# Gated FFT / GEGLU training step: twelve row tiles transposed by DMA, dO scaled on VectorE, the first FFT pieces and sorts spread out

## The chip, the cores and the metric

The kernel runs on 1 core of one Trainium2 chip. The metric is device time in microseconds (us) of one execution, as the median of several runs. The core has TensorE (PE in the profile, its weight loads PEld), VectorE (DVE), ScalarE (ACT), GpSimd (POOL) and SyncE (SP). SP, ACT and POOL can issue DMAs; 16 DMA engines move the data.

## The reference, cut to what matters

Forward and backward of a mix of two branches on one sequence of S = 2048 rows, D = 576 columns, F = 4608:

```python
g = sigmoid((x * gate_w).sum(-1, keepdims=True))
a = irfft2(rfft2(x) * (w_r + 1j*w_i), s=(S, D))            # branch A
b = (gelu(x @ w_gate) * (x @ w_up)) @ w_down               # branch B
out = g * a + (1 - g) * b
# outputs: out and the gradients of x, w_r, w_i, w_gate, w_up, w_down, gate_w for grad_out (dO)
```

Both branches start from `x`, so the gradient of `x` is a sum of both and of the gate's. Everything is bf16 at the borders.

## The kernel before, in words

**Tiles.** The 2048 rows are 16 row tiles of 128 rows; tile t holds rows 16p + t, p being the partition. `xn` and `dB` hold x and dO as loaded (rows on partitions); `xT` and `dOT` hold them transposed (columns on partitions) in five column chunks: chunks 0 to 3 are columns 0 to 511, chunk 4 holds the last 64 columns of two neighbouring tiles, one in each half of the partitions.

**Phase 1** (to about 890 us) is a loop over 18 groups g of 256 columns of F, each in 4 steps m of four row tiles. I count the steps through, step n = 4g + m (`pr` in the code). A step does:

- on PE, `z = dO w_down^T` (L449, L454), then `xy = x [w_gate, w_up]` in two halves (L458, L465);
- on ACT, `da = (1-g) z` (L477), the evacuations of xy (L484 to L487) and the sigmoids of the GELU (L512, or L515 and L516);
- on DVE, the product chain: `H_ew1` (L492 to L496, called as soon as xy is evacuated) and `H_ew2` (L507 to L540: L523 to L533), which waits for the sigmoid. They make `A` and `dH`, which SP stores to DRAM (L537) for phase 2;
- on PE, the weight gradient matmuls of the *group before* (`W_units`, L556 to L619): L577 multiplies `A` with `dB`, L595 and L609 multiply `xn` with `dH`. Their results are evacuated by ACT or DVE (L546) and stored by POOL.

**Way in.** In group 0 the transposes of x and dO are still to be done. `titems` (L396 to L413) gives three items for four row tiles: item 0 transposes column chunks 0 and 1 on PE against an identity (L404, 8 matmuls into PSUM) and copies them to `xT` or `dOT` (L411); item 1 does the same for chunks 2 and 3; item 2 does chunk 4 (L410, 4 matmuls). Step 0 does tiles 0 to 7, step 1 prepares x tiles 8 to 11 (`x1`) and, at its end, dO tiles 12 to 15 (`do2[0]`; the rest of `do2` is done inside the z of the next step, L994 and L1033), step 2 prepares x tiles 12 to 15. `gate(k)` (L423) computes g for four tiles from `xT`; `da` of the same tiles needs it.

**L577 needs dO scaled.** Before the first L577, `dB` is multiplied by 1-g in place, tile by tile (`scale_dB`, L961 to L966). Four tiles are one call: tiles 0 to 3 and 8 to 11 on ACT in step 4 (L1046, L1058), 4 to 7 on DVE in step 4 (L1063), 12 to 15 on ACT in step 5 (L1043). The first L577 come in step 5: two units over tiles 0 to 7 and then the same two over tiles 8 to 15.

**FFT of branch A.** The FFT pieces are spread over the steps: 64 forward pieces for x and dO, `u1` (L639, evacuated by ACT at L642) and `u2` (L653, evacuated by ACT at L659, followed by 17 small DVE operations and a store), then the middle pieces (L758, L836). All of them use the one PSUM tile `pz`, which z uses too. How many have run by the end of a step is set by `want` (L933): for steps 0 to 8 by the table `FIRST` (L930), here 3 by the end of step 7 and 7 by the end of step 8; after that evenly up to step 65. A piece u1 needs its row of x sorted by residue classes (`sort`, L703, one ACT copy of 128x576). The first three sorts are on ACT in step 4 (L1064), the others follow each second piece (L901). The sine tables of the FFT are made by `run_late` in step 6 (L1083): two ACT table loads and seven sines in one row on ACT.

**Queues.** Each engine runs its instructions in the order of the program. SP's DMAs share eight semaphores in rotation with ACT's: the issue of one waits until the DMA eight places before it has landed. At the start SP issues `wdn`, dO tiles 0 to 3, x 0 to 3, the group's two weight blocks, then dO and x alternately, four tiles each; then two small DMAs for a table (L110, L111; the second reads what the first wrote), then the weights of group 1 (`load_w(1, ...)`, L343 to L350, with two DMA transposes of `B_w_down`), then the stores of step 0. The four 64-column tails of group 0's weights are issued from ACT's queue (L345 with `tails`).

**Phase 2** reloads `A` and `dH` by DMA transposes (L1124) and computes b, the gradient of x and the inverse FFT. The change does not touch it.

Of the kernel before, what the change touches and what calls it, by code (L numbers as in the profile page):

```python
# [19 lines left out]
S, D, DF = 2048, 576, 289  # L20
P, T = 128, 16
# [7 lines left out]
FG = 256  # L29
# [8 lines left out]
LO, HI = slice(0, 64), slice(64, 128)  # L38
# [23 lines left out]
def iotas(nc, res, unit):  # L62
    tb = Tables()
    G, V = nc.gpsimd, nc.vector
    kw = dict(allow_small_or_imprecise_dtypes=True)
    tb.halfpi = res.tile([P, 1], F32, name="halfpi")
    V.memset(tb.halfpi[:], math.pi / 2)
    tb.pi = res.tile([P, 1], F32, name="pi")
    V.memset(tb.pi[:], math.pi * EPS_SCALE)
    tb.warm = res.tile([P, 1], F32, name="warm")  # L70
    nc.scalar.activation(tb.warm[:], tb.halfpi[:], ACT.Sigmoid)
    tb.lrow = unit([LQ], F32, name="lrow")
    G.iota(tb.lrow[:], pattern=[[1, LQ]], base=0, channel_multiplier=0, **kw)
    tb.dcol = res.tile([P, 6], F32, name="dcol")
    for k, (r, step, n) in enumerate(((1, 1, 2), (0, 0, 1), (5, -1, 3))):
        k0 = (0, 2, 3)[k]
        G.iota(tb.dcol[:, k0:k0 + n], pattern=[[step, n]], base=r, channel_multiplier=6, **kw)
    tb.late = []
    tb.Rt = []
    return tb  # L80
# [211 lines left out]
def kernel(  # L292
# [4 lines left out]
    nc = tc.nc  # L297
    LD = nc.sync
    ST = nc.gpsimd
# [27 lines left out]
    xT = hres.tile([P, 5, T, P], BF16, name="xT")  # L327
    dOT = hres.tile([P, 5, T, P], BF16, name="dOT")
    xn = wstack.enter_context(tc.tile_pool(name="pxn", bufs=1)).tile([P, T, D], BF16, name="xn")
    dB = wstack.enter_context(tc.tile_pool(name="pdB", bufs=1)).tile([P, T, D], BF16, name="dB")  # L330

    wts = {}

    def load_w(g, part, tails=LD):

        fsl = slice(g * FG, (g + 1) * FG)
        if g not in wts:
            wts[g] = (wpool.tile([P, 5, 2 * FG], BF16, tag="wgu", name="wgu"), wpool.tile([P, 5, FG], BF16, tag="wdT", name="wdT"))
        if part == 0:
            wgu = wts[g][0]  # L340
            for w, c0 in ((B_w_gate, 0), (B_w_up, FG)):
                cols = slice(c0, c0 + FG)
                LD.dma_start(wgu[:, 0:4, cols], w[0:512, fsl].rearrange("(r p) f -> p r f", p=P))  # L343
                for r in (LO, HI):
                    tails.dma_start(wgu[r, 4, cols], w[512:D, fsl])  # L345
        elif part == 1:
            LD.dma_start_transpose(wts[g][1][:, 4:5, :], B_w_down[fsl, DCH[4][0]:D])
            LD.dma_start_transpose(wts[g][1][:, 0:4, :], B_w_down[fsl, 0:512])
        else:
            LD.dma_start(wts[g][1][LO, 4, :], wts[g][1][HI, 4, :])  # L350

    def load_x(t0):
        LD.dma_start(xn[:, t0:t0 + 4, :], x_v[:, t0:t0 + 4, :])
# [10 lines left out]
    load_do(0, 2)  # L364
    load_do(2, 2)
    load_x(0)
    load_w(0, 0, nc.scalar)
    for k in range(1, 4):
        load_do(4 * k)
        load_x(4 * k)  # L370
    tb = iotas(nc, res, unit)

    ew = wstack.enter_context(tc.tile_pool(name="ew", bufs=2))
    keepA = wstack.enter_context(tc.tile_pool(name="keepA", bufs=6))
# [21 lines left out]
    def titems(src, dst, t0, ps, copies, n=4):  # L396

        def item(k, cs):
            def f():
                tp_ = ps[k](BF16).rearrange("p (j t m) -> p j t m", j=2, t=4)  # L400
                for j, c in enumerate(cs):
                    for tt in range(n):
                        if c < 4:
                            nc.tensor.transpose(tp_[:, j, tt, :], src[:, t0 + tt, eo(c)], ident[:])  # L404
                        elif n < 4:
                            for r in (LO, HI):
                                nc.tensor.transpose(tp_[r, 0, tt, :], src[:, t0 + tt, 512:D], ident[:])
                        else:
                            c0 = (t0 + tt) * D + (512, D - P)[tt % 2]
                            nc.tensor.transpose(tp_[:, 0, tt, :], src[:].rearrange("p t d -> p (t d)")[:, c0:c0 + P], ident[:])  # L410
                copies[k](dst[:, cs[0]:cs[0] + len(cs), t0:t0 + n, :], tp_[:, 0:len(cs), 0:n, :])  # L411
            return f
        return [item(k, cs) for k, cs in enumerate(((0, 1), (2, 3), (4,)))]  # L413
# [75 lines left out]
    def H_ew1(g, tiles, da):  # L489
        xb, q, hu = tiles  # L490
        s = ewt("s", g)
        V.tensor_scalar(s[:], q[:], A_GELU, 1.0, op0=ALU.mult, op1=ALU.add)  # L492
        V.tensor_tensor(s[:], xb[:], s[:], op=ALU.mult)
        V.tensor_scalar(q[:], q[:], 6.0 * A_GELU * C_GELU, 2.0 * C_GELU, op0=ALU.mult, op1=ALU.add)
        dH = keep.tile([P, 4, 2, FG], BF16, tag="dH", name="dH")
        V.tensor_tensor(dH[:, :, 0, :], da[:], hu[:], op=ALU.mult)  # L496
        return s, dH
# [187 lines left out]
    xq, gq, graw = {}, {}, {}  # L685
# [17 lines left out]
    def sort(dst, t):  # L703
        if t % 2 == 0:
            classes(dst, t // 2)
        if dst is xq:
            nc.scalar.copy(xq[t], xn[:, t, :].rearrange("p (q r) -> p r q", r=6))
        else:
            nc.scalar.activation(gq[t], graw[t // 2][:, t % 2].rearrange("p (q r) -> p r q", r=6), ACT.Copy, scale=g32[:, t:t + 1])
# [150 lines left out]
    VC, AC = V.tensor_copy, nc.scalar.copy  # L860
# [6 lines left out]
    for c in range(6):  # L867
        w = gwr[0:1, eo(c)] if c < 4 else gwr[0:1, 512:D]
# [58 lines left out]
    mid_at = 4 * T + 8  # L927
    NPR = NT // 2
    LASTP = NG * NPR - 7
    FIRST = (0, 0, 0, 0, 0, 0, 0, 3, 7)  # L930
    done = [0]

    def want(pr):  # L933
# [27 lines left out]
    def scale_dB(k, cp):  # L961
        for t in range(4 * k, 4 * k + 4):
            if cp == AC:
                nc.scalar.activation(dB[:, t, :], dB[:, t, :], ACT.Copy, scale=omg32[:, t:t + 1])  # L964
            else:
                V.tensor_scalar(dB[:, t, :], dB[:, t, :], omg32[:, t:t + 1], None, op0=ALU.mult)  # L966

    for g in range(NG):
# [3 lines left out]
        for m in range(NPR):  # L972
# [14 lines left out]
                H_ew2(g, m, tiles, *state)  # L987
            if g == 0:
                def items(src, dst, t, *cp):
                    return titems(src, dst, 4 * t, (pgtile,) * 3, cp) if t < NPR else [None] * 3  # L990
                do1 = items(dB, dOT, 1, VC, VC, VC) if m == 0 else []
                do2 = items(dB, dOT, m + 2, AC, AC, VC)
                x1 = items(xn, xT, m + 1, AC if m else VC, VC, VC)
# [43 lines left out]
            else:  # L1037
                z, xy_full = H_mm(g, m)
                da = H_da(g, m, z)
                for f in inside:  # L1040
                    f()
                if pr == 5:
                    scale_dB(3, AC)  # L1043
                xy = xy_full(0)
                if held:
                    scale_dB(0, AC)  # L1046
                    held.pop()()
                k0 = int(n > 0 and pr > 6 and ready())
                xy0 = xy
# [6 lines left out]
                    H_act(1, xy, tiles, part)  # L1056
                if pr == 4:
                    scale_dB(2, AC)  # L1058
                elif pr == 6:
                    next(makeB)  # L1060
                state += [*H_ew1(g, tiles, da), da]
                if pr == 4:
                    scale_dB(1, VC)  # L1063
                    for t in range(3):  # L1064
                        sort(xq, t)
                elif pr == 5:
                    build_R(nc, tb, unit, 8)
                    build_R(nc, tb, unit, 12)
                side_work(4.4)
# [378 lines left out]
```

## Time and profile before

| what | us |
|---|---|
| median of the 3 runs | 1370.08 |
| lowest, highest of the runs | 1368.88, 1371.35 |
| the profiled execution, its own time | 1368.51 |
| its span (first to last instruction) | 1366.7 |
| PE busy | 1348.3 (99%) |
| DVE busy | 880.7 (64%) |
| ACT busy | 782.4 (57%) |
| DMA transposes issued by SP: the median time on its queue of L347, L348, L1124, L954, L1157 | 1.26, 1.29, 1.41, 1.64, 3.59 |

The profile is of one execution. Busy time is a union of intervals. PE's matmuls are pipelined: a 128x512 matmul is shown with 379 ns, but one starts every 213 ns; so the time that a wait costs PE is read from start to start and is some 0.16 us longer than the idle that is shown. In the timeline a row gives the start in us from the start of the span, the time that it covers, engine, line, operation and count; in brackets stand the idle time before it and who ended it. In a table of stretches each engine's entry is the busy time in that stretch.

### The profile page before, as it was taken

The numbers are of one execution on the slowest core, as the hardware profiler recorded it, in microseconds if no ns is written. First come the engines' busy times: TensorE is split into PE (matmuls) and PEld (weight loads), VectorE is DVE, ScalarE is ACT, GpSimd is POOL, SyncE is SP. The second block draws the span as 40 slices with busy tenths as digits, with TensorE's granted clock in tenths as the row PEclk, the third lists the DMA queues.
The fourth block names the chain that finished last, engine by engine and source line by source line (L and its number), as shares of the span: only waits on it lengthen the run. The fifth ranks groups of instructions, "written<-read, shape, count | busy, mean of one in ns | idle before, by whom it ended". The sixth has DMA issues, their size and how long they took to land.

```text
span 1366.7 us, 27046 instructions
## 1 busy us (share of the span) xinstructions
PE 1348.3 (99%) x10327; PEld 903.6 (66%) x10408; DVE 880.7 (64%) x2348; ACT 782.4 (57%) x1389; POOL 245.8 (18%) x484
## 2 busy tenths in 40 slices
PE   9999999999999999999999999999999999999999
PEld 7556656656656655656655655658888888888887
DVE  7888988988768876786786655525535443545320
ACT  6987888887767777776776666622332322222210
POOL 2001111111314532442441311100000000000000
PEclk9999999999999999999999999999999999999999
DMA  6424444534634644744654648499999778789773
GB/s 221 121 75 124 130 123 125 154 116 118 168 107 114 175 123 110 184 130 111 182 130 128 157 123 173 126 241 219 217 210 198 175 163 163 165 158 175 158 146 74
DMA packets 487128, 205.33 MB, mean 150 GB/s; under 512 B 306803, under 2 KB 479030, under 8 KB 486998
## 3 DMA queue, kind: packets, MB, share of 16 engines
q1 hardware_dynamic: 460660, 168.75, 53.4%
q0 software_dynamic: 14912, 24.24, 6.1%
q10 hardware_dynamic: 11426, 10.61, 3.3%
q8 instruction: 81, 1.33, 0.4%
q14 instruction: 49, 0.40, 0.1%
HBM read 41.04 MB, written 89.11 MB: 95 GB/s over the span
## 4 chain that ended last, share of the span: by engine, by line
PE 94%; ACT 3%; issue 1%; DVE 1%; DMA 0%; SPq 0%; DVEq 0%; ACTq 0%
PE acc L1198 31%; PE wps L595 17%; PE xy L465 17%; PE wps L577 10%; PE z L449 9%; PE wps L609 2%; PE xy L458 2%; PE z L454 2%; PE acc L1251 1%; PE pf L639 1%; PE acc L1261 1%; PE pf L653 1%; ACT dB L964 1%; PE pf L836 1%; PE pf L758 1%
## 5 line engine op out<-in xcount | busy, mean ns | idle before, releaser
L1198 PEld LDWEIGHTS <-pin 128*128 128x128 bf16 x3456 | 334.8, 98 | 83.2 <-issue 1.1
L465 PE MATMUL xy<-wgu,xT 128*128 128x512 bf16 x1081 | 258.0, 379 | 8.5 <-issue 7.1
L595 PE MATMUL wps<-dH,xn 128*128 128x512 bf16 x1142 | 264.4, 379 | 0.5
L595 PEld LDWEIGHTS <-xn 128*128 128x128 bf16 x1152 | 111.1, 98 | 125.0 <-issue 0.6
L465 PEld LDWEIGHTS <-xT 128*128 128x128 bf16 x1152 | 105.8, 98 | 131.9 <-issue 24.8
L602 POOL DMA_DIRECT2D out_dram<-dw x134 | 73.7, 554 | 429.5 <-ACT dw L546 411.9
L577 PE MATMUL wps<-dB,A 128*128 128x288 bf16 x1152 | 149.8, 286 | 0.5 <-ACT dw L546 0.3
L1198 PE MATMUL acc<-wd_all,pin 128*128 128x288 bf16 x1152 | 146.7, 286 | 0.0
L1198 PE MATMUL acc<-wgT,pin 128*128 128x288 bf16 x1152 | 146.6, 286 | 0.0
L1198 PE MATMUL acc<-wuT,pin 128*128 128x288 bf16 x1152 | 146.0, 286 | 0.0
L1263 ACT ACTIVATE yo<-acc 128x288 bf16<-128x288 f32 x64 | 67.4, 1246 | 133.7 <-PE acc L1261 122.3
L449 PE MATMUL z<-wdT,dOT 128*128 128x256 bf16 x1152 | 137.7, 273 | 0.6 <-ACT ve L659 0.6
L577 PEld LDWEIGHTS <-A 128*128 128x128 bf16 x1152 | 112.0, 98 | 34.1 <-issue 0.9
L477 ACT ACTIVATE da<-z,omg 128x256 bf16<-128x256 f32 x288 | 112.1, 472 | 29.6 <-PE z L454 29.5
L449 PEld LDWEIGHTS <-dOT 128*128 128x128 bf16 x1152 | 112.5, 98 | 22.2 <-issue 1.1
L1379 DVE TENSOR_TENSOR b16t<-acc,f32t 128x288 bf16<-128x288 f32 x32 | 14.6, 458 | 171.7 <-PE acc L1198 171.6
L486 ACT CAST xb<-xy 128x512 bf16<-128x512 f32 x144 | 85.1, 591 | 48.6 <-PE xy L465 48.6
L1253 ACT CAST Z<-acc 98x384 bf16<-98x384 f32 x64 | 27.5, 481 | 106.2 <-PE acc L1251 106.2
L487 ACT CAST hu<-xy 128x512 bf16<-128x512 f32 x144 | 87.4, 607 | 0.0
L484 ACT ACTIVATE q<-xy 128x512 bf16<-128x512 f32 x144 | 80.3, 601 | 3.9 <-PE xy L465 3.5
L523 DVE TENSOR_TENSOR xb<-xb,sg 128x1024 bf16<-128x1024 bf16 x48 | 33.1, 690 | 72.5 <-ACT sg L515 72.5
L546 ACT CAST dw<-wps 128x512 bf16<-128x512 f32 x72 | 42.1, 587 | 59.2 <-PE wps L595 58.6
(514 smaller groups left out, 1825.6 us busy)
## 6 DMA issues: line engine op xcount, KB each, us to landing
scr<-dH SPq DMA_DIRECT2D x144, 256.0 KB, 3.4
scr<-A SPq DMA_DIRECT2D x72, 256.0 KB, 2.4
out_dram<-dw POOLq DMA_DIRECT2D x134, 64.0 KB, 1.9
wd_all<-in_B_w_down_dram SPq DMA_DIRECT2D x3, 1728.0 KB, 13.1
out_dram<-dwd POOLq DMA_DIRECT2D x34, 144.0 KB, 3.1
scr_p<-Vt SPq DMA_DIRECT2D x32, 144.5 KB, 2.8
Vp<-scr_p ACTq DMA_DIRECT2D x32, 144.5 KB, 4.3
wgu<-in_B_w_gate_dram SPq DMA_DIRECT2D x18, 256.0 KB, 3.8
```

What stands on the lines that cost most here:

```text
L449: nc.tensor.matmul(zo(t), lhsT=dOT[:, ci, t, :], rhs=wdT[:, ci, :], start=(t % 4 < 2 and ci == 0), stop=False)
L465: nc.tensor.matmul(xy[k][:, t % 2, :], lhsT=xT[:, ci, t, :], rhs=wgu[:, ci, :], start=False, stop=(ci == 3))
L477: nc.scalar.activation(da[:, t, :], z[:, t % 2, t // 2, :], ACT.Copy, scale=omg32[:, 4 * m + t:4 * m + t + 1])
L484: nc.scalar.activation(q[:, h, :], xy[:, :, 0:FG], ACT.Square)
L486: nc.scalar.copy(xb[:, h, :], xy[:, :, 0:FG])
L487: nc.scalar.copy(hu[:, h, :], xy[:, :, FG:2 * FG])
L546: wcopy[0](out, in_)
L577: nc.tensor.matmul(wps[:, :288], lhsT=tl(0, t)[:, fch * P:(fch + 1) * P], rhs=dB[:, t, h * 288:(h + 1) * 288], start=(t == 0), stop=(t == ...
L595: nc.tensor.matmul(wps[:].rearrange("p a b -> p (a b)"), lhsT=xn[:, t, c * P:(c + 1) * P], rhs=kt[t // 4][1][:, t % 4].rearrange("p k f -> ...
L602: wst[0].dma_start(ov[:, c, fsl], dw[:, k, :])
L1198: nc.tensor.matmul(acc[:, :288], lhsT=src[:, r, :], rhs=w_of(r)[:, h * 288:(h + 1) * 288], start=(first and r == 0), stop=(last and r == F ...
L1263: nc.scalar.activation(yv[:, 3 * b:3 * b + 3], ps[:, 0:288].rearrange("p (r q) -> p r q", r=3), ACT.Copy, scale=(SD2, 1.0)[w])
```

## The change

Five things are altered, all of them in the first steps.

1. Chunks 0 to 3 of x tiles 8 to 11, dO tiles 12 to 15 and x tiles 12 to 15 are no longer transposed on PE: twelve DMA transposes of one row tile each (128 rows, 512 columns), issued by SP from DRAM, write `xT` and `dOT`. Four stand behind the load of x tiles 8 to 11, eight behind that of x tiles 12 to 15. Item 2 (chunk 4) of these tiles stays on PE; items 0 and 1 become empty.
2. The tails of group 0's weights go from ACT's queue to POOL's, behind the first iotas.
3. `scale_dB` of tiles 0 to 3 goes from ACT to DVE (step 4, after `H_ew1`, with 4 to 7), that of tiles 12 to 15 from ACT before the xy of step 5 to DVE after the `H_ew1` of step 5. Tiles 8 to 11 stay on ACT.
4. The first three sorts, on ACT in step 4 before, are on ACT in steps 5, 6 and 7, one each, after the evacuations of xy.
5. `FIRST` asks for 1 FFT piece by the end of step 7 and 3 by the end of step 8, in place of 3 and 7. By `want` the new kernel is 3 pieces behind the old one from step 9 to step 30, 1 behind to step 63 and level from step 64.

```diff
-                for r in (LO, HI):
-                    tails.dma_start(wgu[r, 4, cols], w[512:D, fsl])
+                if tails:
+                    for r in (LO, HI):
+                        tails.dma_start(wgu[r, 4, cols], w[512:D, fsl])
...
-    load_w(0, 0, nc.scalar)
+    load_w(0, 0, None)
+    turned_by_dma = {("x", 2), ("do", 3), ("x", 3)}
+
+    def load_turned(v, dst, k):
+        flat = v[0].rearrange("(p t) d -> p (t d)", t=T)
+        for t in range(4 * k, 4 * k + 4):
+            LD.dma_start_transpose(dst[:, 0:4, t, :], flat[:, t * D:t * D + 512])
     for k in range(1, 4):
         load_do(4 * k)
         load_x(4 * k)
+        for n, v, dst in (("do", grad_out, dOT), ("x", A_x, xT)):
+            if (n, k) in turned_by_dma:
+                load_turned(v, dst, k)
     tb = iotas(nc, res, unit)
+    for w, c0 in ((B_w_gate, 0), (B_w_up, FG)):
+        for r in (LO, HI):
+            ST.dma_start(wts[0][0][r, 4, c0:c0 + FG], w[512:D, 0:FG])
...
-    FIRST = (0, 0, 0, 0, 0, 0, 0, 3, 7)
+    FIRST = (0, 0, 0, 0, 0, 0, 0, 1, 3)
...
-                    return titems(src, dst, 4 * t, (pgtile,) * 3, cp) if t < NPR else [None] * 3
+                    if t >= NPR:
+                        return [None] * 3
+                    its = titems(src, dst, 4 * t, (pgtile,) * 3, cp)
+                    return [gap, gap, its[2]] if ("x" if src is xn else "do", t) in turned_by_dma else its
...
-                if pr == 5:
-                    scale_dB(3, AC)
                 xy = xy_full(0)
                 if held:
-                    scale_dB(0, AC)
                     held.pop()()
...
                 if pr == 4:
                     scale_dB(2, AC)
+                elif pr == 5:
+                    sort(xq, 0)
                 elif pr == 6:
                     next(makeB)
+                    sort(xq, 1)
+                elif pr == 7:
+                    sort(xq, 2)
                 state += [*H_ew1(g, tiles, da), da]
                 if pr == 4:
+                    scale_dB(0, VC)
                     scale_dB(1, VC)
-                    for t in range(3):
-                        sort(xq, t)
                 elif pr == 5:
+                    scale_dB(3, VC)
                     build_R(nc, tb, unit, 8)
                     build_R(nc, tb, unit, 12)
```

`gap` is an empty function; `LD` is SP's queue, `ST` POOL's; `VC` and `AC` are the copies of DVE and ACT.

## The prediction

> **What bounds the kernel now.** I read the page first. Its part 1 gives PE's busy time; in part 2 each digit is an engine's busy tenth in one of 40 equal slices; part 4 gives the engines' shares of the chain that ended last.
>
> ```profile
> PE 1348.3 (99%) x10327; PEld 903.6 (66%) x10408; DVE 880.7 (64%) x2348; ACT 782.4 (57%) x1389; POOL 245.8 (18%) x484
> DVE  7888988988768876786786655525535443545320
> ACT  6987888887767777776776666622332322222210
> ...
> PE 94%; ACT 3%; issue 1%; DVE 1%; DMA 0%; SPq 0%; DVEq 0%; ACTq 0%
> ```
>
> PE is busy all the span and carries the chain. So a change pays only where PE loses time, or where it takes work off PE. I looked for these places with PE's rows, start to start: up to step 8 there are waits; from step 9 to the end of phase 1 the same steps return with the same lengths (12.12, 12.42, 12.83, 14.05 us again and again), which only PE's own work explains. So what follows is about the first 106 us. The same engines by stretch, one row a step (steps 2 to 8; after the stretch PE, PEld, DVE, ACT, POOL busy):
>
> ```profile
> 28.60:37.50 8.90, 8.68 (x96) 5.86 (x95) 7.93 (x16) 8.36 (x17) 0.00 (x0) 1.00 0.30 91
> 37.50:43.50 6.00, 5.84 (x44) 3.33 (x42) 5.74 (x11) 4.77 (x14) 0.00 (x0) 1.00 0.42 131
> 43.50:55.00 11.50, 11.41 (x65) 5.81 (x65) 9.92 (x18) 10.63 (x21) 0.00 (x0) 1.00 0.23 70
> 55.00:67.50 12.50, 11.97 (x80) 7.25 (x80) 10.31 (x20) 12.50 (x22) 2.39 (x4) 1.00 0.68 184
> 67.50:81.10 13.60, 13.39 (x113) 8.95 (x113) 12.32 (x29) 11.65 (x24) 1.63 (x3) 1.00 0.38 115
> 81.10:93.10 12.00, 10.86 (x75) 5.89 (x75) 8.22 (x16) 11.97 (x22) 0.88 (x2) 1.00 0.04 14
> 93.10:105.80 12.70, 11.26 (x87) 6.94 (x88) 12.07 (x42) 10.42 (x18) 1.83 (x4) 1.00 0.32 96
> ```
>
> In step 5 ACT is busy all 12.50 us and DVE 10.31; in steps 7 and 8 PE idles 1.14 and 1.44 us. PE's timeline says for whom:
>
> ```profile
> 28.18 0.61 PE L404 MATMUL pf<-ident,dB 128*128 128x128 bf16 x8
> ...
> 66.40 1.26 PE L577 MATMUL wps<-dB,A 128*128 128x288 bf16 x9 [0.17 <-ACT dB L964]
> ...
> 86.91 0.49 PE L639 MATMUL pf<-Rt,xq 128*96 128x128 bf16 x6 [0.46 <-ACT da L477]
> ...
> 93.09 1.91 PE L449 MATMUL z<-wdT,dOT 128*128 128x256 bf16 x16 [0.63 <-ACT ve L659]
> ...
> 103.04 0.49 PE L639 MATMUL pf<-Rt,xq 128*96 128x128 bf16 x6 [1.39 <-ACT ve L659]
> ```
>
> Step 5 waits for the scaled dO (L964). The waits of steps 7 and 8 (0.46, 0.63, 1.39) are for ACT: its sine tables of step 6 (run_late) make it late, and then every FFT piece needs the one `pz` tile emptied. Start to start the last two are worth 0.79 and 1.55 us.
>
> **The change, part by part.** Times are made against the profiled execution, 1368.51 us (span 1366.7 and 1.8 around it); the runs' median is 1.57 above that, so a difference worked out here is applied to 1370.08.
>
> *Transposes off PE.* The first row of the fence above is one item of 8 transposes: the next matmul starts at 28.62, so it costs 0.44 us. Six items go: 2.7 us, in steps 1 to 3. With them go their waits; PE's idle in steps 1 to 3 is 0.15, 0.22, 0.16, so 0 to 0.5. ACT loses four copies of 1.04, DVE two of about 0.5. I take step 4 to begin 3.2 us earlier, at 40.3 instead of 43.5. It costs DMA work instead: 12 transposes of 128 KB, 512 packets of 256 bytes each; such packets take about 22 ns on one of 16 engines in this trace, so 0.7 us each, 8.4 together. The loads end at about 19.5 now (DMA share falls to 0.41 there), so about 28 with them. The x tiles 12 to 15 are needed by gate(3), which starts at 36.97 now and would at 33.7: 5 us of cover.
>
> *SP's queue.* The 12 issues stand ahead of the two table DMAs and of group 1's weights:
>
> ```profile
> 18.43 0.48 SPq L343 DMA_DIRECT2D wgu<-in_B_w_gate_dram  x1
> ...
> 24.31 1.29 SPq L348 DMA_TRANSPOSE wdT<-in_B_w_down_dram  x1
> ```
>
> An issue with four column blocks takes 1.29, one with 1.5 times the packets (L1124) 1.41: 12 x 1.3 = 15.6, of which some 5 lie in waits for landings that SP has anyway. So group 1's weights start near 29 instead of 18.43; L348, issued at 24.31, landed at 27.63, and lands near 38.5. PE wants it at 40.3. Bounds: nothing if an issue hides in the waits; 12 x 3.59 = 43 us if each is as long as L1157's. I take the row with the nearest size. The stores behind it (L537, step 0 at 28.91) slip by some 8 us; nothing in phase 1 waits for them but the reuse of A and dH buffers (6 and 8 of them).
> L348's eight blocks of 128x128 came in 3.3 us from issue to landing (24.31 to 27.63), 0.4 each; by that row 48 blocks one after another take 20 us, beside PE. [...]
>
> *Tails on POOL.* Four issues of 0.55 us there (the rows L602, L614) before iotas that are wanted at 12 us and done at 3.8; landing wanted at 12.38. ACT is free earlier, but its first copy waits for PE at 5.23. Nothing, either way: POOL then idles 7.3 us, and that is the cover. PE's one DMA wait of the opening (0.87 at 7.75, dO tiles 2 and 3) may shrink; 0 to -0.9, I take 0.
>
> *Scaling on DVE.* ACT loses 8 x 0.67 = 5.3 us in steps 4 and 5, and that ends L577's wait on ACT. What is late next is DVE. Rows of DVE:
>
> ```profile
> 49.12 0.69 DVE L533 TENSOR_TENSOR dH<-dH,xb 128x1024 bf16<-128x1024 bf16 x1
> ...
> 57.33 0.42 DVE L492 TENSOR_SCALAR s<-q 128x1024 bf16<-128x1024 bf16 x1
> ...
> 59.40 1.20 DVE L966 TENSOR_SCALAR dB<-dB,omg 128x576 bf16<-128x576 bf16 x4
> ```
>
> A step of group 0 costs DVE 5.2 us of H_ew2 (from L523 at 52.14 to 57.33) and 2.07 of H_ew1 (57.33 to 59.40); one scaling of four tiles 1.2; H_ew2 of group 1 is 4.94. In the new order DVE must do, before tile 15 is scaled: four H_ew2 of group 0 (20.7), one of group 1 (4.9), five H_ew1 (10.4), three scalings (3.6), two tail copies and a cast (0.9): 40.5 us. It can begin at the sigmoid of step 0:
>
> ```profile
> 24.39 1.04 ACT L411 COPY xT<-pf 128x1024 bf16<-128x1024 bf16 x1
> ...
> 63.53 2.82 ACT L964 ACTIVATE dB<-dB,omg 128x576 bf16<-128x576 bf16 x4
> ```
>
> The first of these ACT rows is the copy that goes, so that L512, at 25.28 now, starts at 24.4 and DVE at 25.45. In between DVE waits twice for a sigmoid, 0.5 together (in step 3 ACT reaches it only after the evacuations of xy). 25.45 + 40.5 + 0.5 = 66.4. Now ACT is done with tile 15 at 66.35 (second row). PE gets there at 61.7, waits for DVE till 66.4 instead of ACT, and then has the last matmul and the second unit's eight left: step 6 begins at 67.6; now at 67.50. **So what steps 1 to 3 win is lost again in step 5**; the net is 0.1. The DMA parts are covered by the same wait: PE may be 2 us late in step 4 without DVE waiting.
>
> *Sorts.* The one of step 5 lies where ACT waits for PE anyway. That of step 6 (0.98; 0.40 of it in ACT's idle before dwd at 77.59) comes ahead of the tables: they and the da of step 7 are about 0.5 later, and L639's wait grows from 0.46 to about 1.0.
>
> *FFT pieces.* Step 7 has u1 alone, step 8 u1 and u2. There is no u2 at the end of step 7 before z, and no pair u2, u1 in the middle of step 8: 0.79 + 1.55 go, and about 0.3 of smaller gaps beside them. The pieces themselves (0.33 and 0.27 us of PE) come later, at the same cost. Later steps have three pieces as they have now, only u1 and u2 change places; I take 0 for that, with bounds of -0.5 and +1.
>
> **Sum:** +0.1 (steps 1 to 6) +0.5 (sort) -2.6 (FFT waits) = -2.0, with -0.2 for the bound of the opening: -2.2. 1368.51 becomes 1366.3, the median 1370.08 **1367.9**.
>
> **Rivals.**
> *DVE keeps up.* If DVE's chain were 3 us shorter (its last step waits less, or the opening moves up 0.9), PE would keep the early gain and lose both waits of step 5: another -3.2: 1364.7. For it: ACT's work there falls by a fifth. Against it: the sum above has 0.5 us of idle in 41.
> *The FFT waits only move.* Three pieces in step 9, u1 and u2 swapped in every step to 30: if in some twenty steps the z after a u2 waits 0.1, the 2.0 are gone: 1369.9. For it: this is just the kind of wait that steps 7 and 8 show. Against it: in the steps now, each of both orders, the last piece lies 1.7 us of matmuls ahead of z, and an evacuation takes 0.66 to 0.82.
> *SP's queue holds up the start (slower).* One mechanism: an issue takes longer while 16 engines are full (L1124's rows reach 2.4, L1157's 3.59). Each 0.1 us per issue makes group 1's weights 1.2 later; the cover is 1.8 until PE and about 3 more in step 5's wait, so from 1.7 us an issue it costs, and from 2 us it outweighs the gain. At 3.59 they land near 63.5: step 4 begins 20 us later than now, less the 2.2: about 1388. Against it: issues of this size took 1.2 to 1.3 even with loads in flight.
> That the code does not do what it says is excluded as far as the order of instructions goes: 96 rows fewer on PE (48 transposes with their loads), L577's four last tiles wait for DVE.
>
> **Numbers.** A change of under 0.2% (2.7 us) can't be told from none. Forecast (1366.6 to 1369.2) 0.47; DVE keeps up 0.20; the FFT waits move 0.23; SP's queue 0.10. A good third of the forecast's own spread lies below 1367.3: faster 0.38, same 0.50, slower 0.12. Eight in ten: 1364.5 to 1371.0, from the middle of the DVE rival to an SP queue that just begins to cost.
>
> **What would show it.** Right: step 4 starts near 40.3; L577 of step 5 waits about 4 us for DVE's scaling, DVE without gaps from 26 to 66; step 6 starts at 67 to 68; L639 of step 7 waits 1 us for da; z of step 8 and the u1 of step 8 wait no more; step 9 starts near 102.5 (now 105.85, of which 1.2 is deferred). Wrong: a wait of L428 or L449 on a DMA in steps 2 to 4, or a step 6 that starts before 66.

## The result and the profile after

| | median us | lowest to highest | runs |
|---|---|---|---|
| kernel before | 1368.41 | 1367.56 to 1371.35 | 20 |
| changed kernel | 1372.46 | 1370.34 to 1375.15 | 20 |

The changed kernel is slower: ratio 1.0027, 95% interval 1.002 to 1.0034. That is 4.05 us, outside the range on record. Of 20 runs the kernel before has a median 1.7 us under that of the three runs that were shown. The profiled execution of the changed kernel took 1370.35 us (span 1368.5), almost its fastest; that of the kernel before (1368.51) is a typical one. So the two traces differ by 1.84 us, and only part of the 4.05 can be read from them.

The page of the changed kernel: part 1 for PE, then the busy tenths of DVE and ACT in 40 slices, then the engines' shares of the chain.

```profile
PE 1355.7 (99%) x10360; PEld 900.7 (66%) x10360; DVE 880.7 (64%) x2353; ACT 772.9 (56%) x1378; POOL 245.1 (18%) x488
...
DVE  7968888888857967876876755525535443545320
ACT  6788887887767776776777666622332322223210
...
PE 94%; DVE 2%; ACT 2%; DMA 1%; issue 0%; SPq 0%; POOL 0%; ACTq 0%; DVEq 0%; POOLq 0%
```

PE's busy time is 7.4 us longer than before although 48 transposes are gone. That is no finding: the trace of before has 10327 matmuls for 10408 weight loads, so 81 records are missing there, and here none (10360 of each). The page tells nothing of where the time went. The steps do. Stretches of steps 3 to 8 (after the stretch PE, PEld, DVE, ACT, POOL busy, then the granted clock):

```profile
33.76:40.70 6.94, 6.23 (x47) 3.26 (x43) 6.49 (x12) 6.13 (x15) 0.00 (x0) 1.00 0.46 104
40.70:51.95 11.25, 11.25 (x64) 5.73 (x65) 10.29 (x19) 7.73 (x16) 0.00 (x0) 1.00 0.74 218
51.95:67.52 15.57, 12.34 (x82) 7.26 (x80) 15.12 (x34) 9.96 (x19) 2.25 (x4) 1.00 0.68 179
67.52:81.10 13.58, 13.58 (x115) 8.95 (x113) 10.34 (x24) 10.29 (x19) 2.16 (x4) 1.00 0.26 75
81.10:91.97 10.87, 10.01 (x64) 5.28 (x62) 6.34 (x12) 10.84 (x20) 0.06 (x1) 1.00 0.18 53
91.97:102.39 10.42, 10.42 (x78) 6.34 (x76) 7.79 (x15) 8.48 (x16) 1.38 (x3) 1.00 0.15 49
```

Step 5 is 15.57 us long (12.50 before), and PE is busy 12.34 of it; DVE is busy 15.12. Step 7 is 10.87 (12.00 before) and step 8 10.42 (12.76 before). The starts of the steps, side by side, in us from the start of the span:

| step | before | changed | difference |
|---|---|---|---|
| 4 | 43.53 | 40.70 | -2.83 |
| 6 | 67.50 | 67.52 | +0.02 |
| 9 | 105.85 | 102.39 | -3.46 |
| 31 | 387.19 | 386.74 | -0.45 |
| 71 (the last of phase 1) | 880.80 | 880.34 | -0.46 |
| end of the span | 1366.7 | 1368.5 | +1.8 |

So the first nine steps went as forecast (step 6 at 67.6, step 9 at 102.5), and the gain was lost in two places that the forecast left at nothing: 3.0 us between steps 9 and 31, and 2.3 us behind step 71. From step 71 to the end it is 485.90 us before and 488.16 after; below I call this stretch **the rest**. PE's waits in the changed kernel, longest in total first:

```profile
PE wps L590 <- DVE dB L979: 3.2, 1, 3.2
...
PE acc L1216 <- DMA wuT<-in_B_w_up_dram: 1.0, 1, 1.0
PE pf L652 <- ACT da L490: 0.9, 1, 0.9
...
PE z L462 <- DMA wdT<-in_B_w_down_dram: 0.7, 1, 0.7
...
PE acc L1216 <- DMA pin<-scr: 0.4, 1, 0.4
```

The first is step 5. The `wuT` and `pin` waits lie in phase 2, at about 1040 us; the kernel before has no such wait. `wuT` (the transposed up weights) is loaded there by nine DMA transposes on SP, one after every three reloads `pin` of the stored activations. First the issues of the kernel before, then of the changed kernel (duration min/median/max in ns, first and last start):

```profile
L1157 SPq DMA_TRANSPOSE wuT<-in_B_w_up_dram x9: 2692/3591/5653, 948.6 to 1027.4; - x9
```

```profile
L1175 SPq DMA_TRANSPOSE wuT<-in_B_w_up_dram x9: 2903/3786/5593, 948.8 to 1031.5; - x9
```

The first of the nine starts at the same time; the ninth 4.1 us later. Counted from the first reload it is issued at 131.0 us before and at 136.1 after.

### The profile page after: what moved, and what is told of

It is laid out like the page before. It is cut to its first block, busy times and chain, and to the rows that moved or that the text cites. A ratio compares the mean times of both kernels' runs of the same rounds, so it can differ in the third digit from the quotient of the medians.

```text
span 1368.5 us, 27031 instructions
## 1 busy us (share of the span) xinstructions
PE 1355.7 (99%) x10360; PEld 900.7 (66%) x10360; DVE 880.7 (64%) x2353; ACT 772.9 (56%) x1378; POOL 245.1 (18%) x488
## 4 chain that ended last, share of the span: by engine, by line
PE 94%; DVE 2%; ACT 2%; DMA 1%; issue 0%; SPq 0%; POOL 0%; ACTq 0%; DVEq 0%; POOLq 0%
PE acc L1216 30%; PE xy L478 17%; PE wps L608 17%; PE wps L590 10%; PE z L462 9%; PE wps L622 2%; PE xy L471 2%; PE z L467 2%; PE pf L652 1%; PE acc L1269 1%; DMA wuT<-in_B_w_up_dram 1%; PE acc L1279 1%; PE pf L849 1%; PE pf L771 1%; PE pf L666 1%; DMA pin<-scr 0%
## 5 line engine op out<-in xcount | busy, mean ns | idle before, releaser
L478 PE MATMUL xy<-wgu,xT 128*128 128x512 bf16 x1152 | 270.5, 380 | 0.0
L590 PE MATMUL wps<-dB,A 128*128 128x288 bf16 x1152 | 150.5, 286 | 3.2 <-DVE dB L979 3.2
L590 PEld LDWEIGHTS <-A 128*128 128x128 bf16 x1152 | 111.8, 98 | 36.8 <-issue 4.0
```

Source lines behind the costliest of these rows:

```text
L478: nc.tensor.matmul(xy[k][:, t % 2, :], lhsT=xT[:, ci, t, :], rhs=wgu[:, ci, :], start=False, stop=(ci == 3))
L590: nc.tensor.matmul(wps[:, :288], lhsT=tl(0, t)[:, fch * P:(fch + 1) * P], rhs=dB[:, t, h * 288:(h + 1) * 288], start=(t == 0), stop=(t == ...
```

## The experiments

Each kernel was timed beside the kernel before on the same chip, and its trace read at the same places. "Ninth" is the issue of the ninth `wuT` load, counted from the first reload. The columns up to "ninth" are of one trace each (the rest is the span, known to 0.1 us, less the start of step 71), the last two of 5 to 30 runs. The first row has the times of the kernel before that were taken beside runs 1 to 4; beside runs 5 to 8 it took 1368.0 (1367.6 to 1370.4), beside runs 9 to 12 1368.2 (1367.3 to 1374.3), and each ratio goes by its own.

| kernel | step 6 | step 9 | step 71 | rest | ninth | median us (lowest to highest) | ratio, 95% interval |
|---|---|---|---|---|---|---|---|
| before | 67.50 | 105.85 | 880.80 | 485.90 | 131.0 | 1368.1 (1367.6 to 1369.0) | |
| changed | 67.52 | 102.39 | 880.34 | 488.16 | 136.1 | 1372.5 (1370.3 to 1375.2) | 1.0027, 1.0020 to 1.0034 |
| changed, again | 68.76 | 103.61 | 881.55 | 487.95 | 136.3 | 1372.3 (1369.3 to 1374.1) | 1.0031, 1.0020 to 1.0041 |
| 12 DMA transposes alone | 64.13 | 102.50 | 877.45 | 488.25 | 136.4 | 1365.9 (1364.6 to 1367.5) | 0.9983, 0.9975 to 0.9992 |
| FFT and sorts alone | 66.34 | 101.20 | 879.17 | 485.93 | 130.5 | 1366.9 (1365.8 to 1369.5) | 0.9992, 0.9983 to 1.0000 |
| changed, scaling on ACT | 64.29 | 99.14 | 877.12 | 487.58 | 136.0 | 1366.4 (1364.2 to 1369.6) | 0.9987, 0.9978 to 0.9996 |
| the same, `FIRST` 1 and 4 | 64.36 | 100.10 | 875.94 | 489.46 | 136.6 | 1365.8 (1364.0 to 1367.4) | 0.9975, 0.9965 to 0.9986 |
| scaling on ACT, 8 transposes | 64.75 | 99.62 | 877.58 | 487.72 | 136.0 | 1365.4 (1364.4 to 1369.5) | 0.9985, 0.9977 to 0.9994 |
| before + 16 unused transposes | 70.42 | 108.78 | 883.73 | 488.07 | 136.4 | 1372.2 (1371.9 to 1374.7) | 1.0036, 1.0023 to 1.0048 |
| before + 4 unused transposes | 66.77 | 105.15 | 880.11 | 485.69 | 132.6 | 1368.0 (1367.5 to 1372.1) | 1.0003, 0.9994 to 1.0012 |
| before, 12 more plain DMAs | 66.88 | 105.26 | 880.21 | 485.69 | 132.3 | 1367.7 (1367.5 to 1368.3) | 0.9997, 0.9988 to 1.0006 |
| before, 12 transposes mid-way | 66.57 | 104.92 | 887.19 | 485.71 | 134.0 | 1376.0 (1374.7 to 1377.7) | 1.0050, 1.0031 to 1.0068 |

The theories at first: **T**, what steps 1 to 3 win is lost in step 5 to DVE's late scaling; its rival, that PE itself or ACT would be just as late. And for the end of the run **P**, that the added transposes leave something behind, against chance and against the new order of the FFT pieces.

**1. The transposes alone.** The kernel before with change 1 only.

> The kernel before with the DMA transposes alone; scaling, sorts, FIRST and the weight tails as before. What happens in the first 110 us: step 4 begins at 40.7 as in the changed kernel. If the early gain was lost to DVE's scaling of dO tiles 12 to 15, it lives here as far as ACT allows: ACT does its two scalings and three sorts from 51 us on and has tile 15 ready at about 62.7, PE gets there at 61.7, so step 6 begins at about 65.2 instead of 67.5 and phase 1 ends some 2.3 us earlier than before. If instead PE itself is slower in steps 4 and 5, step 6 begins near 67.5 here too. What happens behind phase 1: if the twelve transposes leave something behind that makes the DMA stream of phase 2 slower, the stretch from the first reload of phase 2 to the end is 2 to 4 us longer than before and the time is 1368 to 1371; if not, the time is about 2.3 us under the kernel before (1366.1).

Step 6 began at 64.13, 3.4 us before the kernel before and better than the 65.2 expected: ACT was ready. So PE is not slower; the early gain lives if these scalings stay on ACT. It is a gain of its own (ratio 0.9983). But the rest is 488.25.

**2. FFT and sorts alone.** The kernel before with changes 4 and 5.

> The kernel before with the later sorts and FIRST asking for one and three pieces, without the DMA transposes, with the scaling as before. Steps 1 to 4 as before (step 4 at 43.5). ACT loses three sorts in step 4, so tile 15 of dO is ready at 63.6 instead of 66.35 and PE does not wait in step 5: step 6 at 67.2. Steps 7 and 8 lose the waits for the one PSUM tile: step 9 begins at about 102.8 (before 105.85). If the deferred pieces and the swapped order of pieces cost what the changed kernel shows from step 9 to 31 (2.8 us), phase 1 ends 0.1 to 0.6 earlier than before. Phase 2: if its longer time in the changed kernel comes from the twelve transposes, it is as before here and the time is 1368 (same as before); if it comes from the new order of FFT pieces, the time is 2 to 4 us above the kernel before.

Step 9 at 101.20, from there to step 31 it takes 284.37 us (281.34 before): the same 3.0 us are lost as in the changed kernel, with no other part of the change present. The rest is 485.93, as before. So the FFT pieces do not make phase 2 longer.

**3. Scaling back on ACT.** The changed kernel with

```diff
+                if pr == 5:
+                    scale_dB(3, AC)
                 xy = xy_full(0)
                 if held:
+                    scale_dB(0, AC)
                     held.pop()()
...
-                    scale_dB(0, VC)
                     scale_dB(1, VC)
                 elif pr == 5:
-                    scale_dB(3, VC)
```

> The changed kernel with the scaling of dO back where it was: tiles 0 to 3 on ACT in step 4, tiles 12 to 15 on ACT before the xy of step 5. If step 5 waits for DVE alone, DVE now has 2.4 us less, ACT (idle 3.0 us in step 4 and 4.3 us in step 5) has tile 15 ready at about 59.5, before PE gets there at 61.7; the wait of 3.2 us goes, step 6 begins at 64.1 to 64.4 (67.5 in the changed kernel), and phase 1 ends 3.2 us earlier than in the changed kernel. If ACT is the next to be late, step 6 begins at 66 or later. The whole time: 3.2 us under the changed kernel if phase 2 takes as long as there; more or less than that if phase 2's DMA stream moves by itself.

PE's rows at the end of step 5:

```profile
60.37 4.08 PE L590 MATMUL wps<-dB,A 128*128 128x288 bf16 x32
64.29 1.91 PE L462 MATMUL z<-wdT,dOT 128*128 128x256 bf16 x16
```

The 32 matmuls of L590 run without a stop and step 6 begins at 64.29; in the changed kernel they are cut after 20 by 3.23 us. Theory T stands: the wait is DVE's, and 3.2 us of phase 1 hang on it.

**4. The changed kernel again.**

> The changed kernel once more, unaltered, for a second trace and paired times. Phase 1 should end within 0.1 us of the first trace (step 71 at 880.3). If the wait of PE in phase 2 for the DMA-transposed operands (1.0 and 0.4 us in the first trace) is a chance of one execution, the second trace shows another sum there, from 0 to 4 us; if it is fixed by the program, it shows the same 1.4 us at the same place, and then the median (4 us above the kernel before, where the profiled execution is only 1.8 above) stays unexplained by it.

The waits in phase 2 came again, the same sum within 0.2 us, so they are no chance. But phase 1 did not repeat: step 6 began at 68.76, not 67.52, though PE's wait for DVE was shorter (3.01 against 3.23). The stretch of 3.41 us from 65.24 on, first of the first trace, then of this one (PE, PEld, DVE, ACT, POOL busy, granted clock, DMA share, GB/s):

```profile
65.24:68.65 3.41, 3.07 (x23) 2.18 (x23) 3.27 (x9) 1.33 (x3) 0.24 (x1) 1.00 0.16 43
```

```profile
65.24:68.65 3.41, 2.75 (x12) 1.52 (x12) 3.31 (x9) 0.40 (x1) 0.00 (x0) 0.50 0.24 71
```

PE did 23 matmuls in the first and 12 in the second: the granted clock was 0.50 here for just these 3.41 us. The rows of PE in this trace:

```profile
65.90 3.02 PE L590 MATMUL wps<-dB,A 128*128 128x288 bf16 x12 [3.01 <-DVE dB L979]
68.76 1.91 PE L462 MATMUL z<-wdT,dOT 128*128 128x256 bf16 x16
```

The twelve matmuls that were left of step 5 took 3.02 us; in the first trace 2.10. A third trace of the same first steps (run 12) has the half clock at the same place, again for 3.41 us, and step 6 at 68.50. The runs that were only timed show it too, by the mean granted clock of a whole run, which such a stretch lowers by 0.00125 (half of 3.41 us in 1368): it is 1.000 in all 11 runs of kernels 1, 2 and 3 each, and under 1.000 in 17 of the 20 runs of the changed kernel (mean time of those 1372.7; of the other three 1371.1).

The longest wait of the three is the one without the half clock. In both traces that have it the half clock lasted 3.41 us, and in those of before and of the changed kernel's first run, whose spans differ by 1.8 us, the full clock is recorded for 1361.918 us on end in both, 399 times 3.4133. From these lengths I estimate that the clock changes only at marks 3.413 us apart; counted back from the drop at 1368.04, near the end of the first trace, one such mark lies at 64.15, in the wait. The 3.41 us up to this mark, and up to the drops of this trace (65.24) and of run 12 (65.60), columns as above:

```profile
60.74:64.15 3.41, 1.61 (x14) 1.16 (x12) 3.27 (x6) 1.66 (x3) 0.00 (x0) 1.00 0.97 217
```

```profile
61.83:65.24 3.41, 1.06 (x9) 0.70 (x8) 3.27 (x7) 1.09 (x2) 0.00 (x0) 1.00 0.91 247
```

```profile
62.19:65.60 3.41, 0.45 (x5) 0.24 (x3) 3.27 (x8) 0.43 (x1) 0.00 (x0) 1.00 0.89 254
```

PE stood still for 1.80, 2.35 and 2.96 us of these stretches, and the clock was halved at the end of the second and the third. That this idle time decides is an estimate from the three; no run tests it. In other profiled executions a wait of 2.29 us (run 10) went with a mean clock of 1.000, one of 5.8 (run 9) and one of 5.2 us (run 11) with 0.999.

**5 and 6. Transposes whose results nobody uses.** The kernel before, with

```diff
+    turned_by_dma = {("do", 2), ("x", 2), ("do", 3), ("x", 3)}
...
         load_x(4 * k)
+        for n, v, dst in (("do", grad_out, dOT), ("x", A_x, xT)):
+            if (n, k) in turned_by_dma:
+                load_turned(v, dst, k)
```

and the transposes on PE left as they are; in run 6 the set is `{("x", 3)}`.

> The kernel before, with sixteen DMA transposes added whose results are not used: dO and x tiles 8 to 15 are written to their places by DMA and then again by the transposes on PE as before. In the traces so far the nine loads of the transposed up weights in phase 2 (a DMA transpose after every three of the stored activations) come at the same pace in each kernel of a kind: counted from the first reload, the ninth is issued at 131.0 and 130.5 us in the two kernels without the added transposes, at 136.0 to 136.4 in the four with twelve. Theory P (each added transpose slows the later ones, by its packets): 16/12 of 5.3 us, so 138. Theory R (the added ones shift a rotation, which comes round after eight or sixteen): 131. Theory A (any transposes of this kind early in the program, however many): 136. Beside that, group 1's weights start some 20 us later on SP's queue, so step 4 may begin 1 to 3 us later than before (43.5), and the whole time is up by that.

> As the kernel with sixteen unused transposes, with four of them (x tiles 12 to 15). First steps as before within 0.5 us. Ninth load of the up weights, from the first reload of phase 2: theory P (by packets) 132.8; theory R (a rotation) anything, but with sixteen at 131; theory A (any transposes) 136. Whole time: as before if it is at 131 to 133, 1 to 2.5 us above it at 136.

PE's waits from 885 to 1100 us with sixteen, then with four:

```profile
PE acc L1207 <- DMA pin<-scr: 1.2, 2, 1.0
PE acc L1198 <- ACT dw L555: 0.5, 1, 0.5
```

```profile
PE acc L1198 <- ACT dw L555: 0.4, 1, 0.4
```

With sixteen the rest is 488.07, with four 485.69. So nothing of the change but the transposes is needed for the longer phase 2. It does not grow with their number (P by packets wanted 138 and got 136.4) and does not come round after sixteen: four leave it out, and with eight, twelve and sixteen the ninth load is at 136.0 to 136.6.

**7. Twelve plain DMAs.** The loads of dO and x tiles 8 to 15, one DMA a tile.

> The kernel before, with the loads of dO and x tiles 8 to 15 cut into one DMA a tile: sixteen plain DMAs in place of four, so twelve more on SP's queue, same bytes and no transposes added. If the number of DMAs on the queue shifts what comes later, the ninth load of the up weights is issued at 136 us from the first reload, as with the twelve transposes; if it takes transposes, at 131, and the time is the kernel before's within 0.5 us (its first steps may be up to 0.5 us later, for the issues).

Rest 485.69, time as before: more DMAs on the queue do not do it.

**8. Eight transposes.** Kernel 3 with `{("do", 3), ("x", 3)}`.

> The changed kernel with the scaling of dO back on ACT (as in the run before this that had it), and with eight DMA transposes instead of twelve: x tiles 8 to 11 are transposed on PE again. Step 6 begins near 65.2 (64.3 with twelve: two items of eight transposes on PE at 0.44 us each are back). Ninth load of the up weights from the first reload: theory P (by packets) 134.5; theory A (any transposes) 136; theory R (a rotation) something else, 131 if it comes round after eight. Whole time: 1364 to 1365 at 131; 1366 to 1367.5 at 136.

The rest is 487.72 in the trace. The median, 1365.4, is 1.7 us under the profiled execution, though, so in most of its runs the loss is probably small; the spread upward is wide (to 1369.5).

**9. Twelve transposes in the middle.** The kernel before, with

```diff
-            LD.dma_start_transpose(wts[g][1][:, 0:4, :], B_w_down[fsl, 0:512])
+            for _ in range(3 if 6 <= g < 12 else 1):
+                LD.dma_start_transpose(wts[g][1][:, 0:4, :], B_w_down[fsl, 0:512])
```

> The kernel before, with twelve unused DMA transposes in the middle of phase 1 instead of at its start: for groups 6 to 11 the load of the transposed down weights (four column blocks, 256 rows) is issued three times. So far 0 and 4 added transposes left the ninth load of the up weights in phase 2 at 130.5 to 132.6 us from the first reload, 8, 12 and 16 at the start put it at 136.0 to 136.4, and PE then lost 1.7 to 2.4 us in phase 2. If it is the number of transposes on the queue, wherever they stand, it is at 136 here too, phase 2 (from the start of step 71) takes 487.6 to 488.3 instead of 485.9, and the time is about 2 us above the kernel before. If they must stand at the start, or must read x and dO, it is at 131 and the time is as before (phase 1 has cover for them).

The whole time is no answer here: the added loads held up a reload of the FFT, and PE waited for it once, in step 33; the mean clock of this execution is 0.999:

```profile
PE pf L759 <- DMA Vp<-scr_x: 5.8, 1, 5.8
```

That I had not foreseen. The rest, which is the question, is 485.71, so these twelve do no harm to phase 2. They differ from those at the start in more than their place: they read `B_w_down`, 256 rows each. The ninth load is at 134.0, late but not too late.

**10. `FIRST` 1 and 4.** Kernel 3 with one figure changed.

> The changed kernel with the scaling of dO back on ACT (as in the third run) and FIRST asking for 1 and 4 pieces instead of 1 and 3. Now the pieces are an even number (2) behind the kernel before from step 9 to 30, so u1 and u2 keep their places. If the swap of u1 and u2 costs time, four steps of this stretch take 51.42 us as in the kernel before, not 51.74 as in the changed one, and phase 1 ends about 1.3 us earlier than with 1 and 3 (877.1 there, so 875.8): 1.6 us of swap and one deferred piece (0.3) less, one piece (0.3) and perhaps a wait of 0.3 more in step 8. If the swap costs nothing and what is lost after step 9 is the deferred work alone, phase 1 ends at 877.1 again. Phase 2 as in the third run (487.6 from step 71 on).

Steps 10 to 27 have the lengths of the kernel before to 0.01 (14.05, 12.12, 12.42, 12.83), and phase 1 ends at 875.94, as expected. With 1 and 3 the step of 12.12 takes 12.5 to 12.6. In kernel 3, PE's waits from 106 to 390 us have one row that this kernel lacks:

```profile
PE pf L652 <- ACT ve L672: 0.7, 3, 0.2
```

It is the old wait for the one `pz` tile, once in four steps: u1 waits until ACT has emptied it of u2. Three of them are long enough to be listed. In the changed kernel there are five, each 0.31 to 0.40 us from start to start beyond the 0.216 (not 0.213) at which 128x512 matmuls follow each other in these traces (the first two behind the matmuls at 139.17 and 190.91), 1.81 together. By the two kernels the swap of u1 and u2 costs about 1.85 us (2.15 from step 9 to 31, less 0.3 for the piece that now comes in step 8). This kernel has the lowest ratio of the study, 0.9975, though its interval overlaps those of kernels 1, 2, 3 and 8. Its rest is the longest of its kind, and shows a second way in which phase 2 loses time, beside PE's own waits for `wuT` and `pin`. ACT's queue and ACT, then PE:

```profile
1011.53 0.36 ACTq L1324 DMA_DIRECT2D x_t<-in_A_x_dram  x1
1014.49 0.34 ACTq L1324 DMA_DIRECT2D do_t<-in_grad_out_dram  x1
1017.73 0.33 ACTq L1231 DMA_DIRECT2D Vp<-scr_p  x1
1018.11 2.09 ACT L1282 ACTIVATE yo<-acc 128x288 bf16<-128x288 f32 x2 [6.47 <-DMA pin<-scr]
```

```profile
1015.10 0.42 PE L1280 MATMUL acc<-It,Z 98*128 98x96 bf16 x6
1015.36 1.64 PE L1217 MATMUL acc<-wd_all,pin 128*128 128x288 bf16 x12
1019.28 2.98 PE L1217 MATMUL acc<-wd_all,pin 128*128 128x288 bf16 x23 [2.29 <-ACT yo L1282]
```

ACT issues the load of `x_t` at 1011.53; the next two issues follow only at 1014.49 and 1017.73, and the row of `yo` puts the end of its wait down to a `pin` reload, a DMA of SP. In the traces of before and of the changed kernel the issues of SP and ACT use the same eight semaphores, and where the trace tells when the DMA before on the semaphore landed (451 and 456 issues), none starts before that. In the changed kernel ACT's issues at 994.55, 997.35 and 1017.16 stand right behind landings of SP's DMAs on their semaphores, at 994.53, 997.28 and 1017.08. So I take SP to be late here, and ACT's issues with it. Behind them in ACT's order stands `yo`. ACT idles 6.47 us before it; 3.9 of these it would have idled anyway, for PE's results (L1280, done at 1015.52), and 2.6 are the issues'. PE waits 2.29 us for `yo`, the evacuation of a PSUM tile that it needs again.

**11 and 12. The up weights earlier.** Kernel 3, and the changed kernel, with

```diff
-            if i > 2 and wT_loads:
-                load_wuT(*wT_loads.pop(0))
+            for _ in range(2):
+                if i > 2 and wT_loads:
+                    load_wuT(*wT_loads.pop(0))
```

> The third run's kernel (scaling of dO on ACT) with one line of phase 2 changed: the up weights are loaded two parts a job instead of one, so the ninth stands after the fifth job that has one, not after the ninth. SP's queue waits for PE (a free buffer) at most of its reloads there, and the up weights stand behind these waits; so the ninth should be issued some 20 us earlier, PE should not wait for it, and the stretch from step 71 to the end should be 485.9, as in the kernels without the added transposes, in place of 487.6: 1.7 us less in the profiled execution. If the wide spread of the runs (1364.2 to 1369.6 there, 1 us without the transposes) comes from this wait, it shrinks to about 1 us, around 1364.7. If the reloads themselves are late instead, the wait moves to them and nothing is gained.

> The changed kernel as it is, with the same one line of phase 2 altered (two parts of the up weights a job). If its time above the kernel before comes from the late up weights of phase 2, it falls to that of the kernel before or just under it: phase 1 ended at 880.3 and 881.6 in its two traces (880.8 before), so 1367.5 to 1369.5, with a spread of about 1.5 us, from 1372.4 (1370.3 to 1375.2). If the loss sits in phase 1 in most of its runs and the profiled ones only happen to be good there, the median stays above 1370.5.

Both are misses. The ninth load does come early (106.2 and 104.7), and PE no longer waits for it. But kernel 3 goes from 1366.4 to 1373.6 (1.0035, 1.0024 to 1.0045) and the changed kernel from 1372.5 to 1380.2 (1.0074, 1.0053 to 1.0094); the rest is 494.75 and 492.82. PE's and ACT's largest new waits in run 11:

```profile
PE acc L1280 <- ACT bo L1340: 6.1, 2, 5.2
```

```profile
ACT bo L1340 <- DMA pin<-scr: 13.6, 2, 8.5
```

It is the chain of run 10 once more, larger: SP's reloads come later by the loads put before them, ACT's issues wait for them, ACT's evacuations wait behind these, PE waits for ACT; and the mean clock of the profiled execution is 0.999 in run 11 and 0.998 in run 12. So more of SP's stream than the up weights lacks slack there.

## Why the prediction was wrong

**Transposes off PE: right.** 3.2 us by step 4 were forecast. Step 3 begins 3.71 earlier, 0.70 of it from the opening, so 3.0 are the transposes'; step 4 begins 2.83 earlier, for the wait told of next. Whether the opening is the tails' doing can't be said: step 0 begins between 7.1 and 8.6 us in the traces, and between 7.2 and 8.4 in the seven with the tails on ACT.

**SP's queue: right but for a rest.** The issues and what followed:

```profile
6.87 9.30 SPq L374 DMA_TRANSPOSE xT<-in_A_x_dram  x4
...
17.31 6.16 SPq L374 DMA_TRANSPOSE dOT<-in_grad_out_dram  x4
23.51 5.19 SPq L374 DMA_TRANSPOSE xT<-in_A_x_dram  x4
...
30.81 0.47 SPq L343 DMA_DIRECT2D wgu<-in_B_w_gate_dram  x1
...
37.16 1.30 SPq L349 DMA_TRANSPOSE wdT<-in_B_w_down_dram  x1
```

Twelve issues took 20.7 us (15.6 was forecast, some 5 of it in waits that SP has anyway). Group 1's weights start 12.4 us later than before, at 30.81 (10.6 later, near 29, was forecast), and L349 lands at 40.65, where 38.5 was forecast and 40.3 needed: PE waits 0.71 before step 4 (0.4 to 1.5 in the other traces with twelve). Step 5's wait hides it, as foreseen. The 0.4 us a block that the forecast took from L348's row held: the first of the last eight was issued at 17.31 and the last that the trace tells of landed at 28.88, so seven of them, 28 blocks, took 11.6 us, 0.41 a block. In the first steps PE gains by them (run 1 is faster, ratio 0.9983).

**DVE: right to a tenth.** DVE's rows that begin and end its chain:

```profile
24.87 0.69 DVE L536 TENSOR_TENSOR xb<-xb,s 128x1024 bf16<-128x1024 bf16 x1
...
65.17 1.20 DVE L979 TENSOR_SCALAR dB<-dB,omg 128x576 bf16<-128x576 bf16 x4
```

From 24.87 to 66.37, where 25.45 to 66.4 was forecast. The mechanism is right; that the end agrees so closely is luck in part, for the chain began 0.58 earlier, with the earlier opening, and took 41.5 us for 41.0 (DVE waited 1.3 in it, not 0.5). PE waits 3.23:

```profile
59.74 2.61 PE L590 MATMUL wps<-dB,A 128*128 128x288 bf16 x20
65.58 2.10 PE L590 MATMUL wps<-dB,A 128*128 128x288 bf16 x12 [3.23 <-DVE dB L979]
67.52 1.91 PE L462 MATMUL z<-wdT,dOT 128*128 128x256 bf16 x16
...
87.32 0.49 PE L652 MATMUL pf<-Rt,xq 128*96 128x128 bf16 x6 [0.86 <-ACT da L490]
```

Step 6 at 67.52, forecast 67.6. **What the step left out is the clock.** It priced a wait of 4 us on PE at 4 us. The matmuls behind it also ran at half clock (0.50) in runs 4 and 12, which cost 0.9 us in the one and 1.3 in the other (start to start, against the first trace: the twelve of L590 and the 16 behind them). That is seen in two traces of three; the mean clocks, which don't tell the place, allow it in up to 17 runs of 20. The kernel before waits 0.17 there. The rival "DVE keeps up" did not come true; its price, 3.2 us, is what run 3 shows when DVE is spared.

**Sorts: right.** L639's wait (L652 now, last row above) is 0.86; 1.0 was forecast.

**FFT pieces: the step that failed.** "Later steps have three pieces as they have now, only u1 and u2 change places; I take 0 for that, with bounds of -0.5 and +1." The waits of steps 7 and 8 did go, and step 9 began at 102.39 (102.5). But the swap brings the wait back once in four steps, and costs 1.85 us, beyond the upper bound. The rival "the FFT waits only move" had the size, 2.0, and the tile: it spread it as 0.1 over the z of some twenty steps, where five waits of u1 have 0.3 to 0.4 each. With the deferred pieces (1.2) that leaves 0.5 us of the 3.5.

**Phase 2: not in the sum at all.** "What follows is about the first 106 us", and the front of the document says that the change does not touch phase 2. Its instructions are the same. From step 71 on PE's starts are those of the kernel before to 0.01 us, to the end, in the four traces without the loss (runs 2, 6, 7, 9), and in the changed kernel up to about 1000 us. The rest is 2.3 us longer, 1.7 to 3.6 in all seven traces with eight or more added transposes at the start and no other edit to phase 2, and within 0.2 of the kernel before in those four. Shown: that sixteen such transposes are enough without the rest of the change (run 5), that four of them, twelve plain DMAs, or twelve transposes of the weights in the middle are not, and in which ways a late SP stops PE. Not shown: what they leave behind for 800 us; that cause stays open. The number and what they read were not told apart (four of dO and eight of x were not measured), nor was the changed kernel measured with four of them. Nor is the loss of a typical run settled: in runs 1, 5, 8 and 10 the profiled execution was 1.4 to 1.7 us above the median, in the changed kernel 2.1 below it. An estimate from the medians, if phase 1 takes in every run what it took in the profiled one and the rest without loss takes 485.9 (with the 1.8 us around the span): the typical loss is 0.0 to 2.1 us in runs 1, 3, 5, 8 and 10, and -0.2 to 0.1 in runs 2, 6 and 7.

The sum: 1366.3 was forecast for the profiled execution, and it took 1370.35. The 4.05 us between are 1.85 of the swap and 2.25 of phase 2, less 0.05 of smaller misses. The median lies 2.1 above that execution. The half clock in step 5 can be 0.9 to 1.3 of it; the remainder is open. It may lie in phase 2: the middle half of the runs spans 1.5 to 2.5 us in the kernels with eight or more transposes at the start, 0.3 to 0.6 in runs 2, 6 and 7, but also 0.4 to 1.7 in the kernel before. The rival that was to end slower, SP's queue in the first steps, had the right suspect in the wrong place: the 0.71 us that the queue held up PE was hidden by step 5, and it was SP's stream in phase 2 that came too late.

## What to carry to other kernels

Here TensorE's waits of 3.01 and 2.96 us cost 0.9 and 1.3 us more than their length, by a granted clock of 0.50 behind them, and one of 3.23 us at the same place did not. So look at the mean clock of every run, since one trace may be the lucky one. When a shared buffer makes a wait, swapping two users of it at the same count per step is an edit of its own: check each step of the repeating pattern, not the average. And look beyond the stretch that a change touches at any stage that runs with no slack on the same queue, above all where another engine's DMA issues share its semaphores, as ACT's do with SP's here (PE waited 2.29 us behind them in run 10).

## What the runs showed of the hardware that was not expected

- The granted clock fell to 0.50 for 3.41 us in a PE wait of 3.01 us (run 4) and behind one of 2.96 (run 12), and did not in one of 3.23 us at the same place. In the 3.41 us before the two drops PE was idle for 2.35 and 2.96 us.
- Eight to sixteen DMA transposes in the first 30 us went with a stream of DMA transposes 900 us later that was some 5 us behind after 130 us (ninth load at 136.0 to 136.6 against 130.5 and 131.0); the mean time of its 256-byte packets hardly differed (23.2 ns before, 24.2 after), and fewer of them were moved in the 80 us from 55 to 135 us behind the first reload (55,800 before, 52,800 after). Twelve transposes of the weights in mid-run, or twelve plain DMAs, left the rest at 485.7. The cause is not known.
- In run 10 ACT's arithmetic stood still behind late issues on its own queue for 2.6 us, and PE behind it for 2.29.
